# A linear-attention and feed-forward kernel: chunk-end decays turned by four transpositions, and the sixth pair's x turned by TensorE

## The chip, the cores and the metric

The kernel runs on one core of a Trainium2 chip. The metric is device time in microseconds (us), lower is better. The engines are TensorE (PE, matmuls; PEld is its weight load), VectorE (DVE), ScalarE (ACT), GpSimd (POOL, which here issues loads) and SyncE (SP, which here issues stores and DMA transpositions). Each engine works through its own queue in order.

## The reference

```
q, k, v, alpha: (4, 8, 768, 48) float32     # batch, heads, tokens, head size
for t in range(768):
    state = alpha[:, :, t, :, None] * state + einsum('bhd,bhe->bhde', k[:, :, t], v[:, :, t])
    y[:, :, t] = einsum('bhd,bhde->bhe', q[:, :, t], state)
x = y.transpose(0, 2, 1, 3).reshape(3072, 384)
h = x @ w_in                                # (384, 2048)
g = 0.5 * h * (1 + tanh(sqrt(2 / pi) * (h + 0.044715 * h**3)))
out = g @ w_out                             # (2048, 384)
```

A recurrence with a decay for each key feature, and then a two-layer network on the tokens.

## The kernel before, in words

The 768 tokens are cut into 6 chunks of 128, and the 4 batches into 2 pairs: 12 units of work "pair 0" to "pair 11" (pair m is chunk m // 2, batches 2 * (m % 2) and the next). The sixth pair is pair 5. In a name such as `mask4.3` the first number is the pair, the second counts tasks of that kind in it.

For each pair: `load` brings alpha, q, k and v; `ln` (ACT) takes the logarithm of alpha; `cum` (PE) adds it up over the chunk's tokens in PSUM; `b` and `binv` (ACT) are the exponentials of plus and minus the sum; `qp` and `kp` (DVE, L478) are q times b and k times binv. These are turned so that features lie on partitions: by PE and an eviction (`t`, `ev`) for pairs 0 to 4, and by two DMA transpositions on SP's queue (`turn m.0` for q, `turn m.1` for k, L546) from pair 5 on. `attn` (PE, L583, from pair 4 on with the product of q and the carried state in front, L563) gives the chunk's products of q and k, four `mask` tasks (DVE, L590) keep the lower triangle and free its PSUM banks, `y` (PE, L640 or L648) multiplies by v, and `x` (L658 or L664) evicts it. x is turned as well: `tx` (PE, three 128x128 transposes to one half of a pair, L671) and the eviction `xe` (L675), or one DMA transposition for the pair (`turn m.2`, L552).

To carry the state to the next chunk, `kv` (PE, L600) sums k times v, and `st` (DVE, two instructions, L622 and L625) adds the old state and multiplies by the chunk's last decay, `ends` (`end`, L610). For this the last row of b, tokens on partitions, has to come to the features' partitions: one head's 48 features in partitions 0 to 63, the next head's in 64 to 127. In pairs 3 to 9 (`ROW_ENDS`) the task `rows` (DVE, `row_ends`) does that: one transposition of 32x32 blocks in the last 32 partitions, `b_turned`, and four small copies from there into the four quadrants of 32 partitions of a `rows` buffer, of which three exist. Pairs 0 to 2 take it from a small matmul and an exponential, `bend`; pairs 10 and 11, the last chunk, need none.

Block by block the network follows: `l1` (PE, six matmuls, L683) and `gelu` (ACT, L689), eight of each for a pair; `l2` (PE, four matmuls, L702), four for each batch; `ot` (ACT or DVE, L714) evicts and `store` (SP, L727) writes. PSUM is shared by tags: `ff` (four banks: `l1`, `l2`, part of `attn`), `yk` (two banks: `y`, `kv`, `tx`, turned tiles) and `ca` (`cum` and the rest of `attn`). A task that takes a buffer waits for the last user of the one that it replaces.

Nothing is left to the hardware in the order: a planner (`Scheduler.order`) lays out the queues of all engines before the kernel is built. It takes each task's cost from the tables `W` and `COST`, its rank (`prio`), and picks the ready task of the lowest rank within a window of 60 ns. `FIRST` and `LANDED` fix the order up to some 46 us by hand. `SHIFT` adds to single tasks' ranks, and `AFTER` adds dependences; both are lists by name. A change of one cost or rank can thus move tasks on every engine. POOL's queue has `hold` steps in its list of loads: `hold k 6`, for example, makes the loads after it wait until pair 6's turned k has landed.

Of the kernel before, what the change touches and what calls it, by code (L numbers as in the profile page):

```python
# [7 lines left out]
F32 = mybir.dt.float32  # L8
# [8 lines left out]
    cum=530, cum_packed=1500, t8=450, t4=225, attn=340, kv=170, inter=165, intra=203, tx=168, l1_4=655, l1_2=340, l2=651,  # L17
    qk2=880, qk1=500, ev8=610, ev4=350, mask=610, st=1065, st0=545, end=110, attn2=600, vb=320, vb_act=480, ring=1300, ring_issue=670, out=2050, lead=600, receipt=1400, receipt_hw=1000, xc=475, xe=275, ot=540,
    ev8_act=920, ev4_act=520, xc_act=385, xe_act=400, ot_act=450,
    strip=1700, cast=1450, weight=2080, dma=2100, issue=1100, wissue=760, sp=420, store=2600, turn=1250, landed=2200, xbar_qk=1500, xbar_x=1400, turn_lead=50, stored=300, turn_receipt=200, rows=1600, ones=205, late_qk=1700, late_x=1700, late_x6=500, piece=330, late_k=1500, piece_issue=450, begin=620, cast_0=1300, share=1200, cast_1=1900, ln_packed=1040, cold=380, t64=640, fill=216, zero=1100,  # L20
)
COST = {
    ("ACT", "b"): (385, 135), ("ACT", "binv"): (385, 135), ("ACT", "ev"): (600, 40), ("ACT", "gelu"): (510, 110),
# [151 lines left out]
class _Kernel:  # L175
# [37 lines left out]

    TURN_QK = (5, 6, 7, 8, 9, 10, 11)

    TURN_X = (5, 6, 7, 8, 9, 10, 11)

    EV_ACT = (0, 1, 2, 3)

# [14 lines left out]
    PIECES = (0, 192, 320, 384)  # L234

    SHIFT = {
        'cum5.0': 100, 'ev4.1': 97, 'kp6.0': 1515, 'kp9.0': -3, 'kv3.0': -140, 'kv4.1': -540, 'mask3.0': 183, 'mask3.1': 300, 'mask6.3': 2077,
        'qp5.0': 1077, 'qp7.0': 57, 'qp8.0': 110, 'rows4.0': 450, 'rows7.0': -164, 'rows9.0': -280, 'tx3.1': -340, 'tx4.1': -727, 'x6.0': -7088,
        'x6.1': -7042,
    }  # L240

    AFTER = {
        'attn8.0': 'l17.2', 'kv6.1': 'l25.4',
    }

    ROW_ENDS = (3, 4, 5, 6, 7, 8, 9)

    URGENT = (2,)
    BUFS = dict(rows=3, turned=1, ca=1, yk=2, ff=4, la=3, qp=4, kp=4, b8=2, kn=2, qkT=4, atm=6, x=3, ot=4, bend=3, ends=8,
                a=5, q=5, k=5, vb=5)  # L250

    def __init__(self, ctx, tc, q, k, v, alpha, w_in, w_out, out):
        nc = self.nc = tc.nc
        self.tc, self.out = tc, out
        B, H, S, D = q.shape
        self.B, self.H, self.S, self.D = B, H, S, D
        C = self.C = 128
        self.NCH = S // C
        self.src = {"a": alpha, "q": q, "k": k, "v": v}
        self.w_in_dram, self.w_out_dram = w_in, w_out  # L260
        self.d_model, self.d_ff = w_in.shape
        self.NKT, self.NFT = self.d_model // C, self.d_ff // C

        self.const = ctx.enter_context(tc.tile_pool(name="const", bufs=1))
        self.sb = ctx.enter_context(tc.tile_pool(name="sb", bufs=1))
        self.ps = ctx.enter_context(tc.tile_pool(name="ps", bufs=1, space=bass.MemoryType.PSUM))

        const = self.const
        self.ut_h = const.tile([C, C], F16, name="ut_h")
        self.ut = const.tile([C, C], BF16, name="ut")  # L270
        self.gate = const.tile([C, 1], F32, name="gate")
        self.ut_blk = [const.tile([C, C], F16, name=f"ut_blk{i}") for i in range(2)]
        self.blk = const.tile([C, 4], F16, name="blk")
        self.ident = const.tile([C, C], BF16, name="ident")
        self.ones = const.tile([C, 1], F16, name="ones")
        self.zero = const.tile([C, 512], BF16, name="zero")
        self.half = const.tile([C, 2], F32, name="half")
        self.w_in = [const.tile([C, self.NKT, self.d_ff // 4], BF16, name=f"w_in{i}") for i in range(4)]
        self.w_out = const.tile([C, self.NFT, self.d_model], BF16, name="w_out")
        self.state = [[const.tile([C, H // 2, 2 * D], BF16, name=f"st{b}_{i}") for i in range(2)]  # L280
                      for b in range(B)]
        self.ring = {n: [const.tile([C, 2, H, 64], F16 if n == "la" else BF16, name=f"{n}{i}")
                         for i in range(self.BUFS[n])] for n in ("la", "qp", "kp")}
        self.used = {n: 0 for n in (*self.ring, "rows", "b")}
        self.bs = [const.tile([C, 2 * H * D + 16], F32, name=f"b{i}") for i in range(self.BUFS["b8"])]
        self.rows = [const.tile([C, 32], F32, name=f"rows{i}")[:, 0:H].rearrange("f (i p) -> f i p", i=2) for i in range(self.BUFS["rows"])]
        self.NX = 3
        self.xT = [const.tile([C, B, self.NKT, C], BF16, name=f"xT{c}") for c in range(self.NX)]
        self.NG = 2
        self.gT = [const.tile([C, self.NFT, B * C], BF16, name=f"gT{i}") for i in range(self.NG)]  # L290
        self.eng = {"ACT": nc.scalar, "DVE": nc.vector}

    def tile(self, tag, shape, dt, name=None):
        pool = self.ps if tag in ("ca", "yk", "ff") else self.sb
        return pool.tile(shape, dt, tag=tag, bufs=self.BUFS[tag], name=name or tag)

# [133 lines left out]
    def exp(self, u, n, lo, hi):  # L430
        D, H = self.D, self.H

        def emit(e):
# [7 lines left out]
            else:  # L441
                if n not in u:
# [4 lines left out]
                    else:  # L447
                        u[n] = self.sb.tile([self.C, 2, H, D], BF16, tag=n, bufs=self.BUFS["b8"], name=n)
                cum = u["cum"][lo][:, None, 0:H * D] if u["packed"] else u["cum"][:, lo:hi, 0:H * D]
# [4 lines left out]
    def row_ends(self, u):  # L454

        C, H, D = self.C, self.H, self.D
        nc = self.nc

        def emit(e):
            b, t = u["b_row"], self.tile("turned", [C, 2, H // 2, 2, 2, 32], F32, "b_turned")  # L460
            to = u["bend"] = self.rows[self.used["rows"] % len(self.rows)]
            self.used["rows"] += 1
            last = b[C - 32:C]
            nc.vector.transpose(t[C - 32:C].rearrange("t i p o b c -> t (i p o) b c"),  # L464
                                bass.AP(last.tensor, last.offset, [list(last.ap[0]), [D, 2 * H], [32, 2], [1, 32]]))
            for o in range(2):
                nc.vector.tensor_copy(to[64 * o:64 * o + 32], t[C - 32:C, :, :, o, 0, 31])
                nc.vector.tensor_copy(to[64 * o + 32:64 * o + D], t[C - 32:C - 32 + D - 32, :, :, o, 1, 31])
        return emit

    def scaled(self, u, n, lo, hi):
# [133 lines left out]
    def ends(self, u):  # L605
        C, H = self.C, self.H

        def emit(e):
            t = u["ends"] = self.tile("ends", [C, 2, H // 2, 2], F32)
            self.nc.vector.tensor_tensor(  # L610
                t.rearrange("f i p o -> f (i p) o"), u["bend"].rearrange("f i p -> f (i p)")[:, :, None].to_broadcast([C, H, 2]),
                self.half[:, None, :].to_broadcast([C, H, 2]), op=ALU.mult)
        return emit

# [115 lines left out]
    def tasks(self):  # L730
        s = self.s = Scheduler(self.BUFS, self.fill, 40000, self.FIRST, self.LANDED)
        B, NCH = self.B, self.NCH
# [54 lines left out]
        for m, (c, i) in enumerate(pairs):  # L787
# [97 lines left out]
            for j in range(2):  # L885
# [7 lines left out]
                else:  # L893
# [3 lines left out]
                    y.take("yk", xcs[0])  # L897
                if m in self.TURN_X:
                    if j == 0:
# [116 lines left out]
    def run(self):  # L1016
        nc, C = self.nc, self.C
        self.tasks()
        nc.vector.memset(self.zero, 0.0)
        nc.vector.memset(self.ones, 1.0)  # L1020
        make_upper_triangular(nc, self.ut_h, val=1.0, diag=True)
        first = self.p[0, 0]["q"] = self.tile("q", [C, 2, self.H, self.D], F32)
        nc.vector.memset(first[:, 0, 0, 0:1], 0.0)
        make_identity(nc, self.ident)
        nc.vector.memset(self.half, 0.0)
        for o in range(2):
            nc.vector.memset(self.half[64 * o:64 * o + 64, o:o + 1], 1.0)
        nc.vector.tensor_reduce(self.blk, self.ident.rearrange("p (g j) -> p j g", j=4), axis=mybir.AxisListType.X, op=ALU.max)
        same = self.blk[:, None, :].to_broadcast([C, C // 4, 4])
        nc.vector.tensor_tensor(self.ut_blk[1].rearrange("p (g j) -> p g j", j=4), self.ut_h.rearrange("p (g j) -> p g j", j=4), same, op=ALU.mult)  # L1030
        nc.vector.tensor_tensor(self.ut_blk[0], self.ut_blk[1], self.ident, op=ALU.subtract)
        for i in range(max(self.BUFS[n] for n in self.ring)):
            for n in self.ring:
                if i < self.BUFS[n]:
                    nc.vector.memset(self.ring[n][i][:, :, :, self.D:64], 0.0)
        nc.vector.tensor_copy(self.ut, self.ut_h)
        for t in self.rows:
            nc.vector.memset(t, 0.0)
        for t in self.bs:
            nc.vector.memset(t[:, 2 * self.H * self.D:], 0.0)  # L1040
        order = self.s.order()
        for t in order:
            if t.load == LN_EXP:
                self.act_set(LN_EXP)
            t.emit(t.engine)
# [30 lines left out]
```

## Time and profile before

| what | value |
|---|---|
| median of 3 runs | 176.02 us (175.55 to 178.0) |
| the profiled execution's own time | 174.84 us |
| its span, first to last instruction | 173.1 us |
| busy: PE, ACT, DVE, POOL | 166.8, 129.0, 105.2, 60.1 us |
| granted clock of TensorE, mean | 1.000 |
| `b_turned` transpositions L464 | 7, 1241 ns each |
| copies into `rows`, L467 and L468 | 28, 6.0 us in all |
| PE transposes of x, L671 | 30 |
| DMA transpositions of q, of k, of x | 7 each, median 4.5, 5.6 and 2.8 us from issue to landing |

A row of a timeline has the start in us from the span's start, the time that it takes, engine, line, operation, the tiles written and read, their shape and the number of instructions that the row merges; in square brackets stands the idle time of the engine just before, and what ended it.

### The profile page before, as it was taken

The page shows a single profiled execution, that of the slowest core. Times are in us where ns is not written, and L with a number is a line of the kernel's source. Part 1 is how long each engine was busy: PE and PEld are TensorE (multiplying, and loading weights), DVE is VectorE, ACT ScalarE, POOL GpSimd, SP SyncE. Part 2 cuts the span into 40 slices and gives each one's busy share as a digit, 9 for nine tenths or more (in the row PEclk, how much of TensorE's full clock was granted, in tenths as well). Part 3 has the DMA queues.
Part 4 walks back from the last instruction along what each step waited for, and adds up shares of the span by engine and source line. Part 5 has one row for each costly group of instructions (what it writes and reads, how often), then busy time and mean ns, then how long its engine had stood idle before and what let it go on. Part 6 is the DMA issues. An engine that isn't in the chain of part 4 may idle for free.

```text
span 173.1 us, 4474 instructions
## 1 busy us (share of the span) xinstructions
PE 166.8 (96%) x1847; PEld 130.2 (75%) x1847; DVE 105.2 (61%) x220; ACT 129.0 (75%) x212; POOL 60.1 (35%) x71
## 2 busy tenths in 40 slices
PE   7999999999999999999989999999999999999993
PEld 2666999666887795797777787787696796886973
DVE  6399920166889999895995697996950735100000
ACT  4578999756979888869679869868699892581831
POOL 2396446995645500810802503900800300000000
PEclk9999999999999999999999999999999999999999
DMA  4999999999999999799698996999899892401102
GB/s 135 308 252 214 203 241 236 239 228 203 228 301 198 255 238 110 138 204 163 166 246 135 165 218 141 169 252 204 185 174 167 97 177 48 119 18 45 49 0 91
DMA packets 54452, 30.11 MB, mean 174 GB/s; under 512 B 42528, under 2 KB 50848, under 8 KB 54432
## 3 DMA queue, kind: packets, MB, share of 16 engines
q0 software_dynamic: 26464, 17.70, 61.7%
q1 hardware_dynamic: 27424, 11.74, 33.9%
q10 hardware_dynamic: 544, 0.39, 0.9%
q8 instruction: 14, 0.23, 0.6%
q14 instruction: 6, 0.05, 0.1%
HBM read 25.17 MB, written 4.72 MB: 173 GB/s over the span
## 4 chain that ended last, share of the span: by engine, by line
PE 76%; DVE 10%; ACT 6%; DMA 3%; issue 2%; SPq 0%; DVEq 0%
PE hT L683 32%; PE acc L702 28%; PE at L583 3%; DMA a<-in_alpha_dram 2%; DVE b_turned L464 2%; DVE atm L590 2%; PE qkT_ps L488 2%; PE yps L648 2%; DVE stmp L622 1%; DVE st L625 1%; PE kv L600 1%; PE cum L416 1%; PE yps L563 1%; PE idle L318 1%; PE xT_ps L671 1%
## 5 line engine op out<-in xcount | busy, mean ns | idle before, releaser
L683 PE MATMUL hT<-xT,w_in 128*128 128x256 bf16 x576 | 68.2, 273 | 1.1 <-DVE atm L590 0.8
L702 PE MATMUL acc<-w_out,gT 128*128 128x384 bf16 (+3 forms) x416 | 68.8, 314 | 0.0
L689 ACT ACTIVATE gT<-hT 128x512 bf16<-128x512 f32 x96 | 55.4, 602 | 11.7 <-PE hT L683 8.0
L683 PEld LDWEIGHTS <-w_in 128*128 128x128 bf16 x576 | 61.4, 114 | 3.3 <-issue 1.4
L702 PEld LDWEIGHTS <-gT 128*128 128x128 bf16 x416 | 37.2, 98 | 19.6
L590 DVE TENSOR_TENSOR atm<-at,ut 128x512 bf16<-128x512 f32 x48 | 30.3, 683 | 4.8 <-PE at L583 4.6
L714 ACT COPY ot<-acc 128x384 f32<-128x384 f32 (+3 forms) x21 | 9.3, 446 | 17.2 <-PE acc L702 14.6
L351 POOL CAST gate<-qkT 128x1 f32<-128x1 bf16 x6 | 2.1, 353 | 51.4 <-DMA qkT<-kp 51.4
L478 DVE TENSOR_TENSOR kp<-k,binv 128x768 bf16<-128x768 f32 (+1 forms) x15 | 11.9, 793 | 11.0 <-ACT binv L450 10.6
L478 DVE TENSOR_TENSOR qp<-q,b 128x768 bf16<-128x768 f32 (+1 forms) x15 | 11.9, 792 | 8.4 <-ACT b L450 8.4
L337 POOL DMA_DIRECT2D k<-in_k_dram x11 | 12.2, 1108 | 6.0 <-DMA vb<-in_v_dram 3.3
L337 POOL DMA_DIRECT2D q<-in_q_dram x11 | 12.2, 1112 | 4.6 <-DMA k<-in_k_dram 1.2
L337 POOL DMA_DIRECT2D vb<-in_v_dram x11 | 12.3, 1116 | 3.8 <-PE kv L600 1.1
L337 POOL DMA_DIRECT2D a<-in_alpha_dram x11 | 12.3, 1115 | 3.5 <-DMA w_in<-in_moe_w_in_dram 1.3
L450 ACT ACTIVATE b<-cum 128x768 f32<-128x768 f32 (+1 forms) x15 | 10.3, 688 | 2.6 <-PE cum L418 1.5
L309 ACT ACT_TABLE_LOAD x9 | 11.5, 1283 | 0.9 <-PEq L1060 0.7
L689 ACT ACT_TABLE_LOAD x9 | 11.5, 1283 | 0.2
L622 DVE TENSOR_TENSOR stmp<-kv,st 128x384 f32<-128x384 f32 x16 | 8.9, 554 | 3.2 <-PE kv L600 3.0
L450 ACT ACTIVATE binv<-cum 128x768 bf16<-128x768 f32 (+1 forms) x15 | 10.3, 686 | 0.5 <-PE cum L388 0.5
L658 DVE CAST x<-yps 128x384 bf16<-128x384 f32 x9 | 4.9, 556 | 8.2 <-PE yps L648 8.2
L464 DVE STREAM_TRANSPOSE b_turned<-b 32x1024 f32<-32x1024 f32 x7 | 8.7, 1241 | 1.7 <-ACT b L450 1.6
L625 DVE TENSOR_TENSOR st<-stmp,ends 128x384 bf16<-128x384 f32 x16 | 8.9, 558 | 0.6
(86 smaller groups left out, 152.8 us busy)
## 6 DMA issues: line engine op xcount, KB each, us to landing
out_dram<-ot SPq DMA_DIRECT2D x19, 192.0 KB, 3.7
a<-in_alpha_dram POOLq DMA_DIRECT2D x9, 384.0 KB, 8.9
q<-in_q_dram POOLq DMA_DIRECT2D x9, 384.0 KB, 8.6
k<-in_k_dram POOLq DMA_DIRECT2D x9, 384.0 KB, 7.0
vb<-in_v_dram POOLq DMA_DIRECT2D x9, 192.0 KB, 9.6
w_in<-in_moe_w_in_dram POOLq DMA_DIRECT2D x4, 384.0 KB, 9.3
w_out<-in_moe_w_out_dram POOLq DMA_DIRECT2D x4, 384.0 KB, 11.1
out_dram<-ot SPq DMA_DIRECT2D x9, 96.0 KB, 4.6
```

The lines of the kernel that those rows point to most:

```text
L309: nc.scalar.add_instruction(mybir.InstLoadActFuncSet(name=nc.get_next_instruction_name(), act_func_set_id=i, engine=mybir.EngineType.Activ ...
L337: dma(u[t][:, lo:hi].rearrange("t b h d -> t (b h) d"), src.rearrange("b h s d -> s (b h) d")[c * C:(c + 1) * C])
L450: self.nc.scalar.activation(u[n].rearrange("t i h d -> t i (h d)")[:, lo:hi], cum, AF.Exp, scale=1.0 if n == "b" else -1.0)
L464: nc.vector.transpose(t[C - 32:C].rearrange("t i p o b c -> t (i p o) b c"), bass.AP(last.tensor, last.offset, [list(last.ap[0]), [D, 2 * ...
L478: self.nc.vector.tensor_tensor(out, rows, b, op=ALU.mult)
L590: self.nc.vector.tensor_tensor(u["atm", i][:, o], u["at", i][o], self.ut[:, None, :].to_broadcast([self.C, self.H // 2, self.C]), op=ALU.mult)
L622: nc.vector.tensor_tensor(s, acc, old, op=ALU.add)
L625: nc.vector.tensor_tensor(new.rearrange("f p (o d) -> f (p o) d", o=2), acc.rearrange("f p (o d) -> f (p o) d", o=2), ends, op=ALU.mult)
L683: self.nc.tensor.matmul(h[:, s], w_in[:, j, nt % 4 + s], self.xT[c % self.NX][:, lo:hi, j], start=j == 0, stop=j == self.NKT - 1, skip_gro ...
L689: return lambda e: self.nc.scalar.activation(self.gT[c % self.NG][:, nt:nt + 2, lo * self.C:hi * self.C], f.pop(("h", c, lo, nt)), AF.Gelu ...
L702: self.nc.tensor.matmul(f["acc", c, b][:, lo:hi], self.gT[c % self.NG][:, nt, b * self.C:(b + 1) * self.C], self.w_out[:, nt, lo:hi], star ...
L714: self.copy(e)(f["ot", c, b][:, sl], f["acc", c, b] if half is None else f["acc", c, b, half][:, sl])
```

## The change

`row_ends` loses `b_turned` and the copies. Four transpositions take the last 32 partitions of b, each 32 columns out of every second head (even or odd heads, features 0 to 31 or 32 to 63 of what follows), and write into one of the four quadrants of a `rows` buffer, which is now 8 x 32 numbers wide; `ends` reads column 31 of each block. The buffers are no longer zeroed first. `TURN_X` loses pair 5, so its x is turned by two `tx` and two `xe` tasks. The planner's cost of `rows` goes from 1600 to 1400, and `SHIFT` and `AFTER` are new lists, so the queues are laid out anew from about 46 us on.

```
     def row_ends(self, u):
         ...
-            b, t = u["b_row"], self.tile("turned", [C, 2, H // 2, 2, 2, 32], F32, "b_turned")
-            to = u["bend"] = self.rows[self.used["rows"] % len(self.rows)]
+            t = self.rows[self.used["rows"] % len(self.rows)]
             self.used["rows"] += 1
-            last = b[C - 32:C]
-            nc.vector.transpose(t[C - 32:C].rearrange("t i p o b c -> t (i p o) b c"),
-                                bass.AP(last.tensor, last.offset, [list(last.ap[0]), [D, 2 * H], [32, 2], [1, 32]]))
+            last = u["b_row"][C - 32:C]
             for o in range(2):
-                nc.vector.tensor_copy(to[64 * o:64 * o + 32], t[C - 32:C, :, :, o, 0, 31])
-                nc.vector.tensor_copy(to[64 * o + 32:64 * o + D], t[C - 32:C - 32 + D - 32, :, :, o, 1, 31])
+                for half in range(2):
+                    f = 64 * o + 32 * half
+                    nc.vector.transpose(t[f:f + 32], bass.AP(last.tensor, last.offset + o * D + 32 * half,
+                                                             [list(last.ap[0]), [2 * D, H], [1, 32]]))
+            u["bend"] = t[:, :, 31]
...
-    strip=1700, ... rows=1600, ...
+    strip=1700, ... rows=1400, ...
-    TURN_X = (5, 6, 7, 8, 9, 10, 11)
+    TURN_X = (6,7,8,9,10,11)
     SHIFT = {
-        'cum5.0': 100, 'ev4.1': 97, 'kp6.0': 1515, 'kp9.0': -3, 'kv3.0': -140, 'kv4.1': -540, 'mask3.0': 183, 'mask3.1': 300, 'mask6.3': 2077,
-        'qp5.0': 1077, 'qp7.0': 57, 'qp8.0': 110, 'rows4.0': 450, 'rows7.0': -164, 'rows9.0': -280, 'tx3.1': -340, 'tx4.1': -727, 'x6.0': -7088,
-        'x6.1': -7042,
+        'b10.0': 557, 'b6.0': 10, 'b9.0': -173, 'binv8.0': -756, 'kp9.0': -733, 'kv3.1': -567, 'mask3.1': 47, 'mask7.2': -293, 'mask7.3': -104,
+        'mask8.0': 10, 'mask8.1': 43, 'qp6.0': -300, 'qp7.0': 100, 'rows7.0': 100, 'st3.0': 127, 'tx3.1': -30, 'tx4.0': -60, 'tx5.0': 1204,
+        'x7.1': -400,
     }
     AFTER = {
-        'attn8.0': 'l17.2', 'kv6.1': 'l25.4',
+        'cum6.0': 'y4.0',
     }
...
-        for t in self.rows:
-            nc.vector.memset(t, 0.0)
```

What this does to the queues, at the places that the prediction steps through (in the order of each queue):

```
DVE before  rows3 st2.1 mask3.2 mask3.3 end3 mask3.0 mask3.1 | xe3.0 st3.0 rows5 ev4.0 kp5 ev4.1 end5 rows4 mask4.0-4.3 end4 qp5 x4.0 qp6 xe4.0
DVE after   rows3 st2.1 mask3.0 mask3.2 mask3.3 end3 mask3.1 | xe3.0 rows4 st3.0 end4 qp5 ev4.0 kp5 ev4.1 rows5 end5 mask4.0-4.3 x4.1 xe4.0 xe4.1 kp6 qp6
DVE before  st5.1 rows7 mask6.0-6.2 kp7 end7 qp7 mask6.3 x6.0 st6.0 rows8 st6.1 ot5.1 kp8 mask7.0
DVE after   st5.1 kp7 qp7 mask6.0-6.3 rows7 x6.1 end7 st6.0 st6.1 mask7.2 mask7.3 mask7.0 mask7.1 kp8 ot5.1 qp8
DVE before  st8.1 rows9 ot6.1 kp9 qp9 end9 mask8.0      DVE after   st8.1 mask8.2 mask8.3 mask8.0 mask8.1 ot6.1 x8.0 kp9 qp9 rows9
ACT before  ln7 x5.1 ot4.0 b7 binv7 ot4.1               ACT after   ln7 x5.1 ot4.0 xe5.1 b7 binv7 xe5.0 ot4.1
PE before   l23.3 y4 cum6 l23.4 tx4.1 kv4.1 l23.5 tx4.0 PE after    l23.3 l23.4 y4 l23.5 cum6 tx4.0 tx4.1 l23.6
PE before   l15.7 y6 l25.0 l25.1 kv6.0 l25.2 l25.3 cum8 l25.4 l25.5 kv6.1 ... l16.1 attn7
PE after    l15.4 y6 l15.5 l15.6 kv6.0 kv6.1 l15.7 l25.0 l25.1 l25.2 attn7 l25.3 l25.4 l25.5 cum8
PE before   l26.3 cum9 kv8.1 ... l17.3 attn8            PE after    l26.3 attn8
SP before   turn5.1 turn5.0 store3.0 turn6.0 store3.1 turn6.1 turn5.2 store4.0 store4.1 turn7.1 turn7.0 turn6.2
SP after    turn5.0 turn5.1 store3.0 turn6.1 turn6.0 store3.1 store4.0 turn7.1 store4.1 turn7.0 turn6.2
```

POOL's list of loads and holds is the same.

## The prediction

> **What bounds the kernel now.** I read the page's busy shares first, then the stretches of 10 us, then who TensorE (PE) waits for, then VectorE's (DVE) timeline before each of those waits.
>
> ```profile
> span 173.1 us, 4474 instructions
> PE 166.8 (96%) x1847; PEld 130.2 (75%) x1847; DVE 105.2 (61%) x220; ACT 129.0 (75%) x212; POOL 60.1 (35%) x71
> PEclk9999999999999999999999999999999999999999
> ```
>
> ```profile
> 60.00:70.00 10.00, 9.69 (x130) 7.57 (x121) 9.49 (x22) 8.62 (x15) 0.14 (x1) 1.00 1.19 168
> 80.00:90.00 10.00, 9.21 (x114) 7.16 (x113) 8.27 (x16) 7.53 (x13) 3.97 (x4) 1.00 0.91 183
> 100.00:110.00 10.00, 9.83 (x111) 8.01 (x110) 8.65 (x17) 7.92 (x13) 3.45 (x4) 1.00 1.11 157
> 110.00:120.00 10.00, 9.70 (x116) 8.07 (x115) 8.74 (x16) 7.70 (x12) 2.72 (x4) 1.00 1.14 224
> ```
>
> PE is busy 96% of the span at a granted clock of 1.00, so the time is PE's list of work plus its few stalls. The rows of stretches (stretch, its length, then PE, PEld, DVE, ACT, POOL) say where the stalls are. DVE, only 61% busy over all, is at 8.3 to 9.7 of 10 there: late work on DVE is what PE meets.
>
> ```profile
> 67.58 0.86 PE L648 MATMUL yps<-vb,atm 128*128 128x48 bf16 x16
> 69.61 0.33 PE L671 MATMUL xT_ps<-ident,x 128*128 128x128 bf16 x3 [0.18 <-DVE x L658]
> 87.79 1.47 PE L683 MATMUL hT<-xT,w_in 128*128 128x256 bf16 x12 [0.79 <-DVE atm L590]
> 100.18 0.60 PE L583 MATMUL at<-qkT 64*128 64x128 bf16 x15 [0.17 <-DVE ot L714]
> 113.72 0.81 PE L683 MATMUL hT<-xT,w_in 128*128 128x256 bf16 x6 [0.30 <-DVE ot L714]
> ```
>
> Five of six stalls. The first line has no bracket: y4 takes 0.86 us where other groups of 16 take 0.57, so 0.29 lies inside. Bracketed idle time understates a stall, since a matmul's record laps some 0.17 over the next start. By starts (L683 matmuls follow each other every 0.109 us; these two stand 1.061 apart) the stalls cost 0.29, 0.35, 0.95, 0.34 and 0.46, and a sixth, 0.20 at 94.7 (cum8 behind ln8 on ACT): 2.59 us in all. Ahead of 30 us the queues of the compute engines are unchanged; the end (last matmul ends 2.8 us before the span) too.
>
> ```profile
> 84.32 1.24 DVE L464 STREAM_TRANSPOSE b_turned<-b 32x1024 f32<-32x1024 f32 x1
> 85.60 0.16 DVE L467 COPY rows<-b_turned 32x8 f32<-32x8 f32 x1
> 85.77 0.16 DVE L468 COPY rows<-b_turned 16x8 f32<-16x8 f32 x1
> 85.95 0.88 DVE L467 COPY rows<-b_turned 32x8 f32<-32x8 f32 x1
> 86.84 0.17 DVE L468 COPY rows<-b_turned 16x8 f32<-16x8 f32 x1
> 87.04 1.89 DVE L590 TENSOR_TENSOR atm<-at,ut 128x512 bf16<-128x512 f32 x3
> ...
> 110.47 1.24 DVE L464 STREAM_TRANSPOSE b_turned<-b 32x1024 f32<-32x1024 f32 x1
> 111.75 0.16 DVE L467 COPY rows<-b_turned 32x8 f32<-32x8 f32 x1
> 111.92 0.80 DVE L468 COPY rows<-b_turned 16x8 f32<-16x8 f32 x1
> ```
>
> This is `rows7` (then the start of `rows9`): one transposition and four copies, 2.72 us from 84.32 to the masks that free PE's bank. Undisturbed such a group takes 1.98 (59.16 to 61.14). One copy of 0.16 grew to 0.88 here and one to 0.80 at 111.92, while POOL issued loads (at 85.67, 110.43 and 111.57); the transpositions stayed at 1.24 beside the same issues.
>
> **The change, part by part.** (a) *Four transpositions for one and four copies*, in seven pairs (3 to 9). No row has a 32x256 transposition. Lower bound: in proportion, 1241 x 256/1024 = 310 ns, 1.24 for four. Upper bound: each as long as the whole, 4 x 1.24 = 4.96. I take the fixed part from the 32x8 copy, 162 ns, and 1241 - 162 over 1016 elements = 1.06 ns for each element: 162 + 263 = 425 ns alone. Without a chain between them they should follow as masks do (681 ns, one every 598, so 83 saved each time): 4 x 425 - 3 x 83 = 1.45 us, which is near the lower bound. A group saves 0.53, and 0.65 to 0.72 more where a copy was held up: 7 x 0.53 + 1.37 = 5.1 us of DVE. DVE is not the bound, so none of this counts by itself, only in the stalls below. Three preamble memsets (L1038, 17 ns apart) go, long before DVE is needed.
>
> The Trainium skill, in "VectorE: DVE Perf Modes", "The TRN2 errata", speaks against splitting: every instruction with SBUF input pays a fixed extra, so many small ones pay it each time, and it puts the measured fixed term at about 150 cycles. By it, as an estimate, one is (256 + 150)/0.96 = 423 ns and four without overlap 1.69 us, a saving of 0.29 and not 0.53.
>
> (b) *x of pair 5 by PE*: two `tx5` of three 128x128 transposes. `tx` rows advance PE by 0.168 each: +0.34 us, all on the path. One DMA transposition leaves SP's queue (issued at 81.69, 1.21 us, landed 2.74 after). It was ready by 84.43, against 85.50 when PE first used it, so no gain on the path there. Its evictions go to ACT, two of 0.38 (advance): `xe5.1` ahead of `b7`, `xe5.0` ahead of `ot4.1`. `xe5.1` waits for `tx5.1` on PE (near 81.2, with the 0.63 of A and B below) and ACT reaches it at 81.4, after `ot4.0`; so it adds its 0.38 and no wait. Queued behind it are `b7` and `binv7`, and behind those DVE's `kp7`: costed in C. Behind `xe5.0` stands only `ot4.1`, before which ACT idled 1.44 (to 84.89).
>
> (c) *Ranks*: the new queues, stall by stall. Times are before's, minus what was already saved on PE.
>
> A (0.29, y4 on mask4.3). After `kp4` (57.72) DVE now has xe3.0 0.28, rows4 1.45, st3.0 1.15, end4 0.08, qp5 0.87, ev4.0 0.60, kp5 0.87, ev4.1 0.60, rows5 1.45, end5 0.08, with about 0.1 of gaps: the masks start at 65.25 and end 3 x 0.598 + 0.68 later, 67.7. y4 comes one `l2` later: five of 0.65 from 64.98 = 68.2. Free by 0.5. B (0.35, tx4 on x4 behind qp5 on DVE). qp5 is gone from there, x4.1 follows the masks at 68.7 (y4 then ends) and is done by 69.3; tx4 comes after l23.5 and cum6, 69.6. Free by 0.3. PE is 0.63 ahead.
>
> C (0.95, l15.2 on mask6.0 behind rows7). kp7 and qp7, 0.87 each, take rows7's place. st5.1 ends near 83.8 (84.29 - 0.5); kp7's binv7 comes at 83.45 + 0.38 - 0.63 = 83.2; mask6.0 starts at 85.5 and ends at 86.1. l15.2 arrives at 86.83 - 0.63 + 0.34 = 86.5. Free by 0.4. D (0.20): cum8 moves two `l2` (1.3 us) later, gone. E (0.34, attn7's bank on ot5.1, behind rows8 and st6.1): attn7 now goes after l25.2, and needs st6.1. y6 at 88.5, kv6 at 90.2; DVE: mask6.3 to 87.9, rows7 89.4, x6.1 89.9, st6.0 91.6, st6.1 92.7; attn7 at 93.2. Free by 0.5. F (0.46, ot6.1 behind rows9): ot6.1 now goes ahead of rows9. Gone.
>
> So -2.59 and +0.34: -2.25 with nothing new. But the new margins are only 0.2 to 0.5, the closest that of y3.1, whose mask3.3 now has mask3.0 in front: 48.85 + rows3 1.45 + st2.1 1.1 + three masks 1.88 = 53.3, against y3.1 at 53.5. Before had six stalls at such margins. I put two stalls of 0.3 back in, the size of the smaller ones: +0.6. Bounds of this term: 0, and 2.6 (as many stalls as now).
>
> (d) *SP and POOL*. On SP k's transposition of pair 6 goes ahead of q's. POOL's `hold k 6` ends when it lands: 82.75 before. kp6 now follows xe4.1 and starts near 70.7, where it was at 76.03, so q8, k8 and a9 are loaded earlier, and stay out of the way of pair 7's transpositions, which before were issued at 89.86 and 92.32 (the latter lone, 2.76 to land: 95.08). With kp7 and qp7 at 84.5 and 85.4 they are issued some 5 us earlier, and attn7 needs them at 93.2. Nothing else queues behind them but stores.
>
> **Sum.** Profiled execution: 173.1 span + 1.74 around it = 174.84; 174.84 - 2.59 + 0.34 + 0.6 = 173.2. The shown runs' median is 176.02, 1.18 above the profiled one; taken from there it is 174.4, which I take.
>
> **The rivals.** 1. *All stalls go, in every run*: the 1.18 by which the median exceeds the profiled run is more of the same stalls. For: stalls hang on copies that POOL holds up, which vary. Against: no row shows the other runs. 176.02 - 2.25 - 1.18 = 172.6, at the edge of 2%.
>
> 2. *The stalls only move*: margins of 0.3 are eaten by the changed landing times. For: six stalls where before's order was meant to have none. Against: two of them hold disturbed copies that are gone. -2.59 + 0.34 + 2.6 = +0.35: 176.4.
>
> 3. *Slower: the early attentions wait for DMA*. attn7 and attn8 move 6 and 8 us forward. If their transposed q and k land no earlier (95.08 and, issued at 104.36 + 2.74, 107.10), attn7 waits 95.08 - 93.2 = 1.9 and attn8, due at 106.6 (l26.3's end 108.69, less cum9's 0.33, less 2.13 for A to E, plus 0.34), another 0.5: 176.02 - 1.65 + 2.4 = 176.8, slower than before. It decides from a landing of turn7 later than 93.2. For: pair 6's k landed 5.6 us after issue, behind three loads. Against: kp7, qp7 are 4.5 us earlier.
>
> 4. *A transposition costs per instruction*: at 1.24 each, 7 x (4.96 - 1.98) = 20.9 us of DVE against 9.9 idle between 50 and 120: 11 us on PE, 187. It decides from about 0.5 each, when y3.1's 0.2 is gone. Against: the row's proportion to its elements.
>
> **How the numbers follow.** Forecast 0.50; rivals 0.16, 0.17, 0.10, 0.07. Likeliest, 174.4. The range goes from 172.4 (rival 1) to 177.4 (rival 3 with 0.6 more) and leaves out rival 4 and the outer edges. By the bound of 2%, about what a measurement of this kernel can tell from no change (its runs spread over 1.4%): faster (under 172.5), half of rival 1 and 0.04 of the forecast, 0.12; slower (over 179.5), rival 4 and 0.03 of rival 3, 0.10; else 0.78.
>
> **What would show it.** Right: seven groups of four L464-like transpositions of 0.35 to 0.45, 1.4 to 1.6 a group; no copies of `rows`; PE busy about 0.3 more; PE's waits for atm, x and ot under 0.6 in sum; 36 `xT_ps` matmuls. Wrong: a wait of PE's `at` for a DMA into qkT (rival 3), or DVE's busy time up (rival 4).

## The result, and the profile after

| | before | after |
|---|---|---|
| median | 175.79 us (4 runs, 174.72 to 178.0) | 173.34 us (4 runs, 172.88 to 173.65) |
| profiled execution, its own time | 174.84 us | 173.12 us |
| its span | 173.1 us | 171.3 us |

The ratio is 0.9894, with a 95% interval of 0.9866 to 0.9922: 1.1% less time, which is a difference but not one of 2%. The ratios here and below leave disturbed runs out, the medians and ranges don't. The predicted 174.4 us stands 1.1 above the measured median, inside its range.

The page of the changed kernel, with the group of new transpositions:

```profile
span 171.3 us, 4477 instructions
...
PE 165.6 (97%) x1851; PEld 130.3 (76%) x1853; DVE 102.8 (60%) x210; ACT 128.8 (75%) x214; POOL 58.8 (34%) x71
...
L466 DVE STREAM_TRANSPOSE rows<-b 32x256 f32<-32x256 f32 x28 | 12.3, 439 | 0.5
```

DVE did 2.4 us less, not 5.1, and the new transposition takes 439 ns. PE's busy time fell by 1.2 us, although `tx5` was added. Of that, 0.9 lies ahead of 30 us (28.04 to 27.12), where the queues of the compute engines are the same. Behind 30 us it fell from 138.71 to 138.46, with 0.34 of work more. This isn't work that went: the record of a matmul ahead of a stall laps over into it and counts as busy, so fewer stalls also lower this figure. The stretches that the prediction looked at (stretch, length, then PE, PEld, DVE, ACT, POOL, clock, DMA share, GB/s):

```profile
60.00:70.00 10.00, 9.98 (x143) 7.64 (x141) 9.02 (x17) 7.98 (x13) 0.00 (x0) 1.00 1.38 202
80.00:90.00 10.00, 10.00 (x139) 8.13 (x137) 8.55 (x15) 8.85 (x16) 0.26 (x2) 1.00 1.25 219
100.00:110.00 10.00, 10.00 (x113) 7.80 (x110) 8.28 (x18) 7.37 (x12) 6.03 (x7) 1.00 1.19 183
110.00:120.00 10.00, 10.00 (x98) 8.36 (x97) 7.17 (x14) 9.58 (x15) 1.24 (x2) 1.00 0.98 199
```

PE now fills every one of them, where it had 9.21 to 9.83 of 10. DVE is nearly as busy as it was in three of them (in the last 7.17 instead of 8.74); what it does late no longer falls where PE waits for it. The list of PE's waits says the same (line, what it waited for, us in total, times, longest):

```profile
PE k_ps L534 <- ACT qkT L506: 0.5, 1, 0.5
PE qkT_ps L488 <- DVE kp L478: 0.4, 1, 0.4
```

These two are at 10.8 and 8.3 us, ahead of the part that changed, and with two more ahead of 7 us they are all that is listed; `atm`, `x` and `ot` are gone from it. By start distances, the finer measure that the prediction used, the stalls after 30 us add up to 0.50 us, against 2.59 before: 0.18 in y4, 0.20 ahead of kv6 at 90.4, and 0.12 in two more. The y4 group, 0.86 us before:

```profile
68.28 0.76 PE L649 MATMUL yps<-vb,atm 128*128 128x48 bf16 x16
```

The balance of the two profiled spans: stalls -2.09; the start of `cum2` 32.42 to 32.48, +0.06; the rest, span less head and stalls, 138.1 to 138.3, about +0.3 for `tx5` (a span is given to 0.1). Together -1.7 to -1.8, which is 173.1 to 171.3.

### The profile page after: what moved, and what is told of

Read it like the earlier page. It is cut to its first block, busy times and chain, and to the rows that moved or that the text cites. A ratio compares the mean times of both kernels' runs of the same rounds, so it can differ in the third digit from the quotient of the medians.

```text
span 171.3 us, 4477 instructions
## 1 busy us (share of the span) xinstructions
PE 165.6 (97%) x1851; PEld 130.3 (76%) x1853; DVE 102.8 (60%) x210; ACT 128.8 (75%) x214; POOL 58.8 (34%) x71
## 4 chain that ended last, share of the span: by engine, by line
PE 91%; DMA 3%; ACT 3%; DVE 1%; issue 0%; DVEq 0%
PE hT L684 37%; PE acc L703 37%; PE at L583 4%; DMA k<-in_k_dram 3%; PE yps L649 2%; PE cum L416 2%; PE kv L600 2%; PE qkT_ps L488 2%; PE yps L563 1%; PE xT_ps L672 1%; PE yps L641 1%; ACT qkT L506 1%; PE k_ps L534 1%; ACT L309 1%; PE qkT_ps L519 1%; PE idle L318 1%
## 5 line engine op out<-in xcount | busy, mean ns | idle before, releaser
L690 ACT ACTIVATE gT<-hT 128x512 bf16<-128x512 f32 x96 | 54.1, 604 | 5.7 <-PE hT L684 2.6
L351 POOL CAST gate<-qkT 128x1 f32<-128x1 bf16 x6 | 1.1, 189 | 50.2 <-DMA qkT<-kp 50.2
L450 ACT ACTIVATE b<-cum 128x768 f32<-128x768 f32 (+1 forms) x15 | 10.3, 684 | 5.3 <-PE cum L416 3.4
L466 DVE STREAM_TRANSPOSE rows<-b 32x256 f32<-32x256 f32 x28 | 12.3, 439 | 0.5
L450 ACT ACTIVATE binv<-cum 128x768 bf16<-128x768 f32 (+1 forms) x15 | 10.2, 683 | 2.2 <-PE cum L416 2.1
L399 ACT ACTIVATE la<-a 128x768 f16<-128x768 f32 (+1 forms) x11 | 8.7, 787 | 0.1
```

Source lines behind the costliest of these rows:

```text
L450: self.nc.scalar.activation(u[n].rearrange("t i h d -> t i (h d)")[:, lo:hi], cum, AF.Exp, scale=1.0 if n == "b" else -1.0)
L466: nc.vector.transpose(t[f:f + 32], bass.AP(last.tensor, last.offset + o * D + 32 * half, [list(last.ap[0]), [2 * D, H], [1, 32]]))
L690: return lambda e: self.nc.scalar.activation(self.gT[c % self.NG][:, nt:nt + 2, lo * self.C:hi * self.C], f.pop(("h", c, lo, nt)), AF.Gelu ...
```

## The experiments

Each kernel was compared with the kernel before in the same series of runs, so the ratios are what to compare; the medians belong to their series. The theories that the expectations name are these. S: what counts is how late DVE's work is at the places where PE meets it, so each kernel's time follows from its stalls. R: the new order of the queues alone brings the gain. P: the cheaper decays alone bring it. N: DVE's work is hidden, and its length matters little. For the copies, H: what costs is that a copy is held up beside POOL's loads; L: what costs is the length of the group.

**The changed kernel again** (e0), without any edit.

> The changed kernel itself, once more beside the other three. Every theory: 173.3 us +- 0.5, ratio to before 0.985 to 0.993, PE stalls after 30 us 0.4 to 0.7 in sum (0.45 in the first profile).

Measured: 173.28 us (172.86 to 173.91, 6 runs), ratio 0.9889 (0.9842 to 0.9937), stalls 0.47. The result repeats.

**New queues, old decays** (e1): exactly the changed kernel's queues, with one transposition and four copies in each group.

```
-                for half in range(2):
-                    f = 64 * o + 32 * half
-                    nc.vector.transpose(t[f:f + 32], ...)
+            nc.vector.transpose(t[C - 32:C]..., ...)            # 32x1024, as before
+            for o in range(2):
+                nc.vector.tensor_copy(to[64 * o:64 * o + 32], t[C - 32:C, :, :, o, 0, 31])
+                nc.vector.tensor_copy(to[64 * o + 32:64 * o + D], t[C - 32:C - 32 + D - 32, :, :, o, 1, 31])
```

> The changed kernel's queues, order for order, but the chunk-end decays by one transposition and four copies as before (1.98 us a group against 1.80). Theory S (stalls: what counts is how late DVE's masks, x and evictions are where PE meets them): two groups of rows stand in front of y4 (2 x 0.18), one each in front of y3.1 and kv6 (0.18 each), and one or two copies are held up 0.7 beside loads, of which some 0.3 reaches PE: +0.7 to +1.2, 174.0 to 174.5, ratio to before 0.990 to 0.993. Rival R (the new queues alone bring the gain, the form of the decays nothing): as the changed kernel, 173.3. Rival P (the cheaper decays bring it): back near before, 175.5.

Measured: 175.29 us (174.65 to 176.07, 6 runs), ratio 1.0003 (0.9953 to 1.0053). The new order by itself brings nothing, and R falls. S had the direction, but its range (0.990 to 0.993) was missed, since the stalls come to 3.53 us, the longest of them 1.50. DVE's timeline of this kernel shows where that one is made, in the group of pair 6:

```profile
75.85 1.24 DVE L464 STREAM_TRANSPOSE b_turned<-b 32x1024 f32<-32x1024 f32 x1
77.12 0.93 DVE L467 COPY rows<-b_turned 32x8 f32<-32x8 f32 x1
78.07 0.17 DVE L468 COPY rows<-b_turned 16x8 f32<-16x8 f32 x1
78.25 0.17 DVE L467 COPY rows<-b_turned 32x8 f32<-32x8 f32 x1
78.43 0.78 DVE L468 COPY rows<-b_turned 16x8 f32<-16x8 f32 x1
79.23 2.48 DVE L590 TENSOR_TENSOR atm<-at,ut 128x512 bf16<-128x512 f32 x4
```

POOL's timeline beside it:

```profile
76.89 1.18 POOL L337 DMA_DIRECT2D q<-in_q_dram  x1
78.03 1.17 POOL L337 DMA_DIRECT2D k<-in_k_dram  x1
```

And PE's, which needs those masks:

```profile
79.98 1.30 PE L702 MATMUL acc<-w_out,gT 128*128 128x384 bf16 x7 [1.34 <-DVE atm L590]
```

A held copy ends when POOL's issue ends: 77.12 + 0.93 = 78.05 against 76.89 + 1.18 = 78.07, and 78.43 + 0.78 = 79.21 against 78.03 + 1.17 = 79.20. The two copies that start less than 0.23 us after the second issue's start go through in 0.17. The prediction's own rows of before read the same way once one looks for it: loads were issued there at 85.67 and 111.57 and take 1.16 and 1.15, and the long copies end at 86.83 and 112.72. In all, the two traces have seven copies that start 0.23 us or more into an issue with more than their own 0.17 of it left, and all seven end with it (the shortest took 0.33); the five that start 0.22 or less into one take their usual 0.16 to 0.17. In e1 the copies are held for 2.6 us in all (14 of a mean of 261 ns and 14 of 255, against 166 undisturbed), in the kernel before for 1.35. The largest part of that is pair 6's: the new order has loads issued from 76.89 to 79.17, beside its group.

**Old queues, new decays** (e2): exactly the queues of before, with x of pair 5 by DMA; only `row_ends`, its buffers and `ends` are the changed kernel's.

```
-            nc.vector.transpose(t[C - 32:C]..., ...)
-                nc.vector.tensor_copy(to[...], ...)             # four of them
+                    nc.vector.transpose(t[f:f + 32], ...)       # four of 32x256
```

> Before's queues, order for order, x of pair 5 by DMA as before, but the chunk-end decays by four transpositions (1.80 us a group instead of 1.98, and 2.72 and 2.61 for rows7 and rows9). Theory S, from the stalls of before: 0.29 and 0.35 go (two groups in front, 0.36 earlier), 0.95 shrinks to 0.06 to 0.1 (rows7 0.9 shorter), 0.34 to 0.16, 0.46 goes (rows9 0.8 shorter), 0.20 stays: -1.9 to -2.2, 173.7 to 174.2 from the median of before, ratio 0.988 to 0.992. Rival R (queues alone): 175.5 or more, ratio over 0.997. Rival P: as the changed kernel less its 0.34 on PE, 173.0.

Measured: 174.44 us (172.78 to 179.09, 6 runs), ratio 0.991 (0.9836 to 0.9984), stalls 0.88. As S said, and by this number P too: nearly all of the 1.1% is there without the new order, though the interval is wide.

**Old decays whose copies can't be held** (e8, e10). e8 is e1, and e10 is the kernel before, with each copy written as the maximum of a value with itself, which leaves the same numbers.

```
-                nc.vector.tensor_copy(to[64 * o:64 * o + 32], first)
-                nc.vector.tensor_copy(to[64 * o + 32:64 * o + D], rest)
+                nc.vector.tensor_tensor(to[64 * o:64 * o + 32], first, first, op=ALU.max)
+                nc.vector.tensor_tensor(to[64 * o + 32:64 * o + D], rest, rest, op=ALU.max)
```

> e1 again (the changed kernel's queues, one transposition and four small operations), but each of the four small copies is a maximum of the same operand with itself: same numbers, same bytes, same count, but a two-input instruction and not a copy. Theory H (e1's 2.0 us are mostly copies held up beside POOL's loads, 0.58 at 49.76, 0.93 at 77.12 and 0.78 at 78.43 in its profile, and this holds up copies only): no instruction of a group over 0.25, groups of 2.0, the stall of 1.50 at 78.4 and the 0.57 at 53.3 go; 0.37 at y4, 0.38 at kv6 and some 0.2 at y3.1 stay: stalls 1.0 to 1.3 against 3.53, 173.7 to 174.2. Rival L (it is the length of the group and its five instructions in a chain): as e1, 175.3.

> The kernel before with the same maximum in place of each copy, all else as before. Theory H: rows7 goes from 2.72 to 2.0 and rows9 from 2.61 to 2.0, so of the 2.59 of stalls 0.95 becomes 0.2 to 0.3 and 0.46 goes: -1.1, ratio to before 0.992 to 0.996; longer executions by late DMA transpositions stay as frequent as before. Rival L: ratio 1.00, as before.

Measured: e8 173.47 us (173.18 to 174.15, 7 runs), ratio 0.9918 (0.9885 to 0.9951), stalls 1.64; e10 174.51 us (12 runs), ratio 0.9938 (0.9905 to 0.9972). The `rows` tile of e8 (count, then the least, middle and greatest duration in ns):

```profile
L468 DVE TENSOR_TENSOR rows<-b_turned x14: 164/167/169, 49.3 to 115.5; 32x8 f32<-32x8 f32 x14
L469 DVE TENSOR_TENSOR rows<-b_turned x14: 164/170/172, 49.5 to 115.7; 16x8 f32<-16x8 f32 x14
```

None of 28 is longer than 172 ns, where the copies in the same queues reached 934. Only three of them start 0.23 us or more into a load's issue, though (at 103.82 to 104.19, of one from 103.58 to 104.73), and pair 6's group has no issue beside it here. e10 has seven more, all at 172 ns or less. Its `rows9` stands where the copy of before took 0.80, 0.35 into an issue; DVE's row and POOL's:

```profile
110.79 0.17 DVE L469 TENSOR_TENSOR rows<-b_turned 16x8 f32<-16x8 f32 x1
```

```profile
110.44 1.15 POOL L337 DMA_DIRECT2D a<-in_alpha_dram  x1
```

In the same profile l15.2 waits 0.25 where it waited 0.95, and the 0.46 ahead of 113.72 is gone, as H said. (That execution took 175.99 us, above e10's median; it has one wait that is none of these, 2.73 us at 138.24 for a DMA transposition of x that landed 10.3 us after its issue.) The group is as long as an undisturbed one of before, yet most of the gain is there. So H holds, and L falls as the sole cause; but e8's stalls of 1.64, above H's 1.0 to 1.3 and the changed kernel's 0.5, leave the length a part. The runs of the two orders and three forms together, as ratios to the kernel before:

| decays | queues of before | changed kernel's queues and `tx5` |
|---|---|---|
| one transposition, four copies | 1 | 1.0003 (e1) |
| one transposition, four maxima | 0.9938 (e10) | 0.9918 (e8) |
| four transpositions | 0.991 (e2) | 0.9894, 0.9889 (after, e0) |

Going down, the first step, which only takes the hold-ups away, is by the middle values the large one: 0.6% in the left column, 0.85% in the right. The second, 0.3% in both, is not separated by the intervals, nor is any step to the right.

The profiles, one execution each, say the same. The start of `cum2`, ahead of where the queues part, varies from 31.6 to 32.7 us; the time from there to the end of the span, in us, is

| decays | queues of before | changed kernel's queues and `tx5` |
|---|---|---|
| one transposition, four copies | 140.6 | 141.7 (e1) |
| one transposition, four maxima | 139.5 (e10, less its wait of 2.73) | 139.8 (e8) |
| four transpositions | 138.9 (e2) | 138.8, 138.8 (after, e0) |

By these single executions the hold-ups are worth some 1.1 us in the old queues and 1.9 in the new ones, the shorter group 0.6 and 1.0, and with four transpositions the new queues and `tx5` together nothing.

**A shorter and a longer group** (e7, e6). e7 transposes half the columns; it leaves the decays of each pair's second batch out, and the buffers are zeroed at the start in their place. e6 does each group of four twice.

```
e7  -  nc.vector.transpose(t[f:f + 32], ... [2 * D, H] ...)
    +  nc.vector.transpose(t[f:f + 32, 0:H // 2], ... [2 * D, H // 2] ...)
e6  -  for o in range(2):
    +  for o in (0, 1, 0, 1):
```

> The changed kernel with the four transpositions at half the width (32x128 instead of 32x256): the decays of each pair's second batch are left out. It prices the instruction: two points, 1241 ns at 1024 elements and 439 at 256, give 1.044 ns an element and 172 ns fixed, so 306 ns at 128 and 1.25 us a group instead of 1.80 (in proportion to the elements it would be 220). Theory S: only the 0.45 of stalls that are left can go: 172.9 to 173.3. Rival P (time follows DVE's busy time in the crowded stretches): 7 x 0.55 = 3.9 us less DVE, 1 us or more off, under 172.4.

> The changed kernel with each group of four transpositions done twice (28 more, 1.78 us more for each of seven pairs, 12.5 us of DVE in all; the second four write the same numbers again). Theory S: a group more is paid where the margin behind it is less than it: y3.1 1.7, y4 some 2, y5 1.2, kv6 1.7, later pairs 0 to 1: +6 to +8, 179 to 181. Rival N (DVE, 60% busy, hides it): under +1, 174.3.

Measured: e7 172.68 us (172.15 to 172.86, 4 runs), ratio 0.9863 (0.9829 to 0.9898), stalls 0.42; e6 183.53 us (183.11 to 184.08, 4 runs), ratio 1.0499 (1.0452 to 1.0546), stalls 10.8. The page's group in e7:

```profile
L466 DVE STREAM_TRANSPOSE rows<-b 32x128 f32<-32x128 f32 x28 | 8.5, 305 | 0.5
```

The three sizes now in rows, 305 ns at 128 elements, 439 at 256 and 1241 at 1024, lie on one line: (1241 - 439) / 768 = 1.044 ns for each element and 172 ns fixed. e7 takes 3.8 us of DVE's work away and gains some 0.6 us by the medians, not separated by the intervals, for few stalls are left to take; it lies between what S and P said. e6 adds 7 x 1.78 = 12.5 us and loses 10.2 against the changed kernel's median (10.6 by the ratios): nearly all of it comes through, more than S's 6 to 8, and N falls. DVE is idle for 40% of the span, but hardly where these groups lie.

**New decays and pair 5 by PE under the old ranks** (e5): `row_ends` and `TURN_X` of the changed kernel; `SHIFT`, `AFTER` and the cost of `rows` as before, so that the planner lays the queues out anew.

```
-    TURN_X = (5, 6, 7, 8, 9, 10, 11)
+    TURN_X = (6, 7, 8, 9, 10, 11)
(and row_ends as in e2)
```

> Both parts of the change (four transpositions, x of pair 5 by PE), but the planner with before's ranks, dependences and its cost of 1600: before's queues with the two tx and xe of pair 5 put in and a few neighbours moved. Theory S: as e2 plus 0.34 for tx5, 174.0 to 174.6, ratio 0.990 to 0.994. Rival R (queues alone): 175.8 or more. Rival P: 173.3, as the changed kernel.

Measured: 175.37 us (174.66 to 175.99, 6 runs), ratio 1.0006 (0.9955 to 1.0057), stalls 3.08. S's range was missed. PE's timeline:

```profile
87.80 4.09 PE L684 MATMUL hT<-xT,w_in 128*128 128x256 bf16 x36 [1.01 <-DVE atm L590]
99.05 1.47 PE L684 MATMUL hT<-xT,w_in 128*128 128x256 bf16 x12 [0.89 <-DMA xT<-x]
```

`rows7` is still ahead of pair 6's masks, and a new wait, for a DMA transposition of x, appears. So the two parts under ranks that were not made for them give nothing, while the decays alone, in e2, gave nearly everything: the new ranks and `tx5` work only together (the next experiment has the ranks without `tx5`), and the runs show no gain of theirs over e2.

**The changed kernel with x of pair 5 by DMA** (e3): the same queues, written out, without `tx5` and its evictions, and with the transposition on SP after `x5.1`.

```
-    TURN_X = (6,7,8,9,10,11)
+    TURN_X = (5, 6, 7, 8, 9, 10, 11)
```

> The changed kernel's queues, order for order, but x of pair 5 turned by one DMA transposition on SP right after its second half is there (some 81.7 us), and without the two tx and the two xe. Theory S: PE saves 0.34, but in the new queues the loads q8, k8 and a9 are issued at 76.6 to 80.1 and land at 85.2 to 88.5, and a DMA transposition lands behind the loads issued ahead of it (turn7.1: issued at 85.0, landed at 89.5, 1.0 after a9). So x of pair 5 lands at 86 to 89, where l15.0 needs it at 85.35: 0.6 to 3 us of wait for DMA xT, 173.6 to 176.0. Rival (only PE's work counts): -0.34, 173.0.

Measured: 177.8 us (177.39 to 179.59, 4 runs), ratio 1.0181 (1.0092 to 1.0269). SP's queue and then PE's:

```profile
81.17 1.28 SPq L552 DMA_TRANSPOSE xT<-x  x1
```

```profile
88.94 3.36 PE L684 MATMUL hT<-xT,w_in 128*128 128x256 bf16 x16 [3.89 <-DMA xT<-x]
```

Issued at 81.17, behind loads that POOL issued at 76.8 to 79.1, x had landed 7.7 us later; before, the same transposition took 2.74. PE stood for 3.89 us and then ran at half the clock, as the stretches show (clock in the third column from the end):

```profile
84.00:89.00 5.00, 1.11 (x35) 0.82 (x34) 4.94 (x9) 1.76 (x2) 0.00 (x0) 1.00 1.11 202
89.00:95.00 6.00, 6.00 (x53) 4.99 (x53) 1.23 (x3) 3.31 (x6) 3.62 (x4) 0.72 1.15 156
```

S's range, up to 176.0, was too low: the wait is longer than its 0.6 to 3 us, and the half clock wasn't in it. So in the new order `tx5`, 0.34 us on PE, spares some 4.5 us: 177.8 against 173.3 by the medians (the ratios, 1.0181 and 0.9889, are 5 us apart).

**The two late groups split** (e9): `rows5` and `rows7` of the changed kernel in two halves, the second half behind `x4.1` and `x6.1`, so that pair 4's and pair 6's later work is 0.9 us sooner.

```
-  rows5.0 end5.0 mask4.0 ... mask4.3 x4.1            rows7.0 x6.1 end7.0
+  rows5.0/0 mask4.0 ... mask4.3 x4.1 rows5.0/1 end5.0    rows7.0/0 x6.1 rows7.0/1 end7.0
```

> The changed kernel, but rows5 and rows7 done in two halves of two transpositions, the second half moved into gaps of DVE: rows5's behind x4.1 (DVE idles 0.58 there), rows7's behind x6.1. All else in the changed kernel's order. From its profile the masks of pair 4 end 0.9 earlier (stall of 0.18 in y4 gone) and x6.1 starts as soon as y6 is there (stall of 0.20 in front of kv6 gone): stalls 0.1 instead of 0.47, -0.35 against the changed kernel, 172.9, ratio 0.985 to 0.989. Rival: the moved halves delay xe4 or st6 by 0.3 and give it back, 173.3.

Measured: 172.99 us (172.55 to 173.43, 6 runs), ratio 0.988 (0.9845 to 0.9915), span 170.8. The stalls of y4 (0.56 for the group) and ahead of kv6 are gone. But `xe4` now comes behind the moved half, and kv4 waits for it: 0.35 us, of which 0.26 lie ahead of this row and the rest inside:

```profile
70.40 0.59 PE L604 MATMUL kv<-vb,kp 128*128 128x96 bf16 x8
```

From the start of `cum2` to the end it takes 138.8 us, as the changed kernel does. So this profile speaks for the rival, that the moved halves give it back. Its median is the lowest of the complete versions, but its 0.3 us against the changed kernel are within the intervals.

## Why the prediction was right, and where it was not

*What bounds the kernel.* Held. PE's work stayed but for `tx5`, most stalls went, and the span followed them to 0.1 us.

*(a) The transpositions.* The duration held: 425 ns estimated, 439 measured (435 to 444). The overlap of 83 ns did not. The masks' overlap doesn't carry over:

```profile
64.23 1.79 DVE L466 STREAM_TRANSPOSE rows<-b 32x256 f32<-32x256 f32 x4
66.15 2.48 DVE L590 TENSOR_TENSOR atm<-at,ut 128x512 bf16<-128x512 f32 x4
...
85.73 2.48 DVE L590 TENSOR_TENSOR atm<-at,ut 128x512 bf16<-128x512 f32 x4
```

Four of them take 1.79, which is 4 x 439 with small gaps, so a group saves 0.18 and not 0.53. The prediction's other estimate, 1.69 a group by the Trainium skill, "VectorE: DVE Perf Modes", "The TRN2 errata", was nearer: a fixed part that is paid each time. The hold-ups, 1.37 us there, were listed as DVE time with no worth of their own. They were the larger part of the gain by the middle values: e10, and e8 against e1, which take away them alone, have 0.6 to 0.85%, of 1.1%.

*(b) `tx5`.* Held: about +0.3 on PE by the balance above, with no wait of PE behind its evictions. What the step didn't price was the alternative. It compared `tx5` with the DMA as it was in the old order (ready at 84.43, needed at 85.50); beside loads that come earlier, as e3 shows, that transposition costs some 4.5 us.

*(c) The ranks, stall by stall.* B to F went as worked out: mask6.0 ended at 86.41 (86.1 predicted) ahead of l15.2 at 86.8; st6.1 was done at 93.26 (92.7) ahead of attn7 at 93.7 (93.2). A went only in part. With two groups 0.35 longer than estimated, which is 0.7 of the 0.9, mask4.3 ended at 66.15 + 2.48 = 68.63 instead of 67.7, and 0.18 of the 0.29 stayed in y4; e9, which takes half a group out of the way there, has none of it left. The wrong step is what the ranks were credited with: all 2.59 us. The steps put the shorter groups into the new order, but not into the old one, and so never asked what the decays alone would do there. e2 has the old order and 0.88 us of stalls; e1 has the new order and 3.53. e2's ratio is 0.991 without any of the new order, so the forecast was in part lucky: its number did not need the step that most of its working is about.

*New stalls.* 0.6 us assumed, as two of 0.3. Measured 0.50 in all: the rest of A (0.18), one of 0.20 at kv6, two of 0.12 together.

*(d) SP and POOL.* kp6 at 70.89 (70.7 predicted), and q8, k8 and a9 issued 76.61 to 78.90. But they were not out of the way of pair 7's transpositions. SP's queue of the changed kernel, with the later of the two:

```profile
86.96 1.50 SPq L546 DMA_TRANSPOSE qkT<-qp  x1
```

It landed at 92.06, 5.1 us after its issue, where 2.76 had been seen for one issued alone. attn7 at 93.7 found it there by 1.7 us. Rival 3 did not happen, but came within 1.1 us of the 93.2 from which it counts.

*The sum.* From profile to profile -1.72 us, against -1.65 predicted. The medians fell by 2.45. The term that was off is the one carried over by hand: the 1.18 us by which the median of before stood above its profiled execution was left in the forecast, while after it is 0.22 (173.34 against 173.12). Of the 1.1 us by which the forecast was too high, this is 0.96. That term stood on three runs, 175.55 to 178.0. In the longest later series, of 18 runs, the median of before is 175.04, only 0.20 above its profiled execution (in the two shorter ones it is 175.31 and 176.13), so most of the 1.18 looks like the choice of runs and not like a property of the kernel. Rival 1 read it as more of the same stalls, held copies above all. No profile shows that: e10's, at 175.99 us, has no held operation and a late DMA transposition instead. What sets the runs of before apart stays open. Rival 1's other half, no stall left at all, did not come either.

*The other rivals.* 2 (the stalls only move, 176.4): no, though e1 and e5 are such kernels. 4 (1.24 us per transposition, 187): no, 172 ns fixed and 1.044 for each element. e6 supports its working, since DVE's surplus does come out on PE.

*The checks it named.* Transpositions of 0.35 to 0.45, no copies, PE's waits for `atm`, `x` and `ot`: as said. A group of 1.4 to 1.6: wrong, 1.80. "PE busy about 0.3 more": a wrong check, since that figure also holds the head and the laps into stalls, as said with the page.

## What to carry to other kernels

When a small instruction is sometimes several times its usual length, look at what the neighbouring engine does when it ends; here another form of the same copy, without any new order, took some 0.6% of the 1.1%. Test an order and an operation apart and together: the new queues were worth nothing with the old copies, no more than the old ones with the new decays, and some 4.5 us worse without PE's turn of x. Price a shorter operation at the places in the queue where the bound engine waits behind it, and add the landing margins of the transfers that an earlier operation releases.

## What the runs showed of the hardware

Small fp32 copies from SBUF to SBUF on DVE, 0.16 us alone, took 0.33 to 0.93 when they started 0.23 us or more into one of POOL's load issues, and ended when the issue ended (seven of seven in before and e1); five that started 0.22 or less into one were not held. Neither were two-input maxima of the same size (ten that far into an issue in e8 and e10, 172 ns at most) nor transpositions (six such in the changed kernel, 441 at most). The Trainium skill, "SBUF — State Buffer", "SBUF: two separate sides", says that DVE and GpSimd share a port pair as an exclusive lock, that a DVE operation in a two-port mode needs it, as an fp32 copy does, and that whichever starts first keeps the other waiting for the whole instruction. Its box on loads tells of the load that waits for the copy; the rows here show the copy waiting for the load, but not from the issue's very start. That the lock is the cause is the page's reading; the runs show only which forms are held.

After 3.89 us without a matmul the granted clock was 0.5 for 3.41 us in e3 (0.72 as the mean of 89 to 95), by the trace's record of the clock, which cost another 1.7 us (half of 3.41) beside the wait. In e1 a wait of 1.34 left PE's clock as it was. The Trainium skill, "TensorE: Matmul & The Clock Gate", Part 1, gives an idle window of about 3.4 us before the clock falls to half and as long a busy one before it comes back, which agrees.

A transposition of 32 partitions in fp32 costs 172 ns and 1.044 ns for each element of a partition, from 128 to 1024 of them, and four in a row don't overlap (1.79 us for 4 x 439 ns).
